# Own buffers for the loads of maxima and of parts, later places for both, and two up-projections ahead of the first scores, in an attention block followed by a mixture of 4096 single-row experts

## The chip, the core and the metric

One core of a Trainium2 chip runs one program. Its engines work side by side and are ordered only by semaphores: PE multiplies matrices (PEld is its weight load), DVE and ACT do element-wise work from the on-chip memories SBUF and PSUM, POOL does element-wise work in SBUF, and SP issues DMA transfers, in order, between device memory and SBUF. The metric is the device time of one execution in microseconds (us).

## The reference, cut to what matters

2048 tokens of 448 features; 16 attention heads of 28; then, for each token and each of 16 heads, the best 8 of 64 x 64 experts, each of which is one row of u (what to multiply with) and one row of v (what to add).

```python
h = x + attention(layernorm(x), wqkv) @ wo
xf = layernorm(h)
q = jnp.einsum("nd,dhc->nhc", xf, w_q)               # two halves, q1 and q2
s1, s2 = q1 . k1, q2 . k2                            # 64 scores each
...                                                  # best 8 of each, then best 8 of the 64 sums
g = _softmax(top_s, axis=-1)
act = _gelu(jnp.einsum("nd,nhkd->nhk", xf, u[top_e]))
h2 = h + jnp.einsum("nhk,nhk,nhkd->nd", g, act, v[top_e])
```

## The kernel before, in words

The 4096 experts are not gathered: all 32 slices of 128 experts are computed for every token, and a dense table G of gate weights picks. Products in fp16 use two planes (a high part and a rest), so each needs 11 matmuls of 128x512 (`mm_all`, line 92, over `products`). u and v are brought to such planes in the kernel: `tops` loads each of the 32 slices (`raw`) and DVE takes its largest absolute value (line 141); `share` makes one scale of them; `part` loads a slice again (`raw`, line 1039), lets POOL scale and split it (`hl`, lines 1044 to 1048) and SP store it (`us` or `vs`, line 1051).

Four stages follow one another.

1. To about 150 us: layer norm, q, k and v (`pq`).
2. Attention, 256 units, one for each of 4 token blocks, 4 groups of 4 heads and 16 key tiles: 12 matmuls S (line 556), two exponentials on ACT (P, line 560), 4 product groups A (line 583). Other work is woven in by `weave`: each generator has a number of steps and a stretch of positions, and the next step is taken from the one whose position is lowest; one position is one unit. The first 68 units carry the folding of the key matrices and `tops` of u. In the second stretch, positions 0 to 189, from about 318 to 843 us (so 2.8 us a position), lie for the token blocks b = 0, 1, 2: the output projection and second layer norm (`project(b)`, positions 5 to 31, 65 to 91, 127 to 153), the expert scores and the best 8 of each (`search(b)`, the 33 positions after; ACT writes the scores to `fresh`, DVE takes maxima and indices, line 809 and 811, into `ti`), then the best 8 of the sums (`pairs_of`, partly on POOL, `sel`, lines 866 to 883; its DVE half is `cand`, `ts`, `pos`). Beside these run the parts of u (positions 0 to 50), the maxima of v (6 to 66), their `share` (67 to 70), and the parts of v (74 to 180). A tile pool keeps so many buffers (`bufs`) for a name; here `raw` has 6, for maxima and parts together.
3. Behind attention, about 843 to 938 us: `project(3)`, the scores of block 3 (`kept_scores`, into `ring`), and G for block 0 (`weights(0)`: DVE makes one-hot tiles `f`, `fg`, `p`, PE sums them, line 1014, ACT copies into G, line 1016). Then `load_X(0)` brings back the layer-normed tokens of block 0.
4. The experts, block after block: `up` (11 matmuls `A<-XHb,u`, line 92, a Gelu into one of four `ring` buffers, line 1170), `weigh` (DVE `ring`, line 1184, ACT `w`, line 1185, DVE `w`, line 1186) and 12 matmuls `acc<-v,w` (line 1211) for each of 32 slices f. Beside block 0 runs `later`: `pairs_of` for what was left of block 2, the best 8 of block 3, then `soften` (`ex`, line 893, `sl`, line 905 and 906), whose `sl` PE transposes (line 917); and then `weights(1)` (line 1004).

In stages 2 and 3 the written order is the order of each engine (`manual_schedule`). In stage 4 a scheduler orders the instructions by its own estimates, so a change of what is ready there moves rows on DVE, ACT and PE.

Of the kernel before, what the change touches and what calls it, by code (L numbers as in the profile page):

```python
# [10 lines left out]
F32 = mybir.dt.float32  # L11
# [17 lines left out]
XS = 2.0 ** 11  # L29
LS = 2.0 ** 11  # L30
TOP = 14
ONE = 2.0 ** 15
QS = 2.0 ** 2 / (XS * 2.0 ** TOP)

# [26 lines left out]
def block(ctx: ExitStack, tc: tile.TileContext, x, wqk, wv, wo, wq, k12, uT, v, cst, out):  # L61
# [565 lines left out]
    X = {}  # L627

    def project(b, offset=6, room=None):

        X[b] = XH, XL = bx.tile([128, 4, 512], F16, name="XHb"), bx.tile([128, 3, 512], F16, name="XLb")
# [80 lines left out]
    PROJECT = 26  # L712

    def load_X(b):
        X[b] = XH, XL = bx.tile([128, 4, 512], F16, name="XHb"), bx.tile([128, 3, 512], F16, name="XLb")
        nc.sync.dma_start(XH, x_d[b][:, :4])
        nc.sync.dma_start(XL, x_d[b][:, 4:])

# [48 lines left out]
    def search(b, order):  # L767


        loads = {}  # L770
        heads = [i for n, (i, j) in enumerate(order) if not n or order[n - 1][0] != i]

        def load(n, k):

            if n < len(heads):
                loads[n, k] = w = sp.tile([128, 4, 4, 128], F16, name="w", bufs=3)
                nc.sync.dma_start(w, wp_d[heads[n]][:, k])

        load(0, 0)
        load(0, 1)  # L780
        load(1, 0)
        yield
        last = None
        g = 0
        for n, (i, j) in enumerate(order):
            if last:
                best(*last)
            turned = n + 1 == len(order) or order[n + 1][0] != i
            src = sp.tile([128, 512], F32, name="fresh", bufs=3)
            nc.scalar.activation(src, scores_of(*X[b], (loads[g, 0], loads[g, 1]), j, turned), AF.Identity, scale=gscale[:, i:i + 1])  # L790
# [233 lines left out]
    def tops(S, src, cols):  # L1024

        raw = {}
        for k in range(36):
            if k < 32:
                raw[k] = sp.tile([128, 512], F32, name="raw", bufs=6)
                nc.sync.dma_start(raw[k][:, :cols], src(k))  # L1030
            if k >= 4:
                S.see(k - 4, raw.pop(k - 4)[:, :cols])
            yield

    TOPS = 36

    def part(S, src, dst, cols, planes):
        raw = sp.tile([128, 512], F32, name="raw", bufs=6)
        nc.sync.dma_start(raw[:, :cols], src)
        yield  # L1040
        yield
        hl = sp.tile([128, planes, 512], F16, name="hl", tag=f"hl{planes}", bufs=5 if planes == 2 else 3)
        r, h = raw[:, :cols], [hl[:, k, :cols] for k in range(planes)]
        nc.gpsimd.tensor_scalar(r, r, S.scale, 1.0, op0=OP.mult, op1=OP.mult)  # L1044
        nc.gpsimd.tensor_copy(h[0], r)
# [25 lines left out]
    with tc.manual_schedule(engines={ET.PE, ET.DVE, ET.Activation, ET.Pool, ET.SP}):  # L1071
# [20 lines left out]
        places = pp.tile([128, 8, 16 * H], F16, name="places", bufs=1)  # L1092
        for k in range(8):
            nc.gpsimd.memset(places[:, k], float(k))
        r2 = ExitStack()
        wo_p = r2.enter_context(tc.tile_pool(name="wo_p", bufs=1, reuse_waits="tile"))
        w2 = r2.enter_context(tc.tile_pool(name="w2", bufs=2, reuse_waits="tile"))
# [3 lines left out]
        for b in range(3):  # L1101
# [24 lines left out]

    us = {}

    def load_u(f):
        u = be.tile([128, 2, 4, 128], F16, name="u")  # L1130
        nc.sync.dma_start(u.rearrange("p k t e -> p k (t e)"), us_d[f])
        return u

    with tc.manual_schedule(engines={ET.PE, ET.DVE, ET.Activation, ET.Pool, ET.SP}):
        room = {"xt": [ring[4 * j + 2] for j in range(4)], "at": [ring[3], ring[7]]}
        pools = [tc.tile_pool(name="sw0", bufs=1, side="right", reuse_waits="tile")]
        with ExitStack() as c1:
            pools = [c1.enter_context(pools[0])]
            sc = kept_scores(3, pools)
            weave((project(3, 2, room), 12, 0, 0.25), (islice(sc, 1), 1, 0.02, 0.03),  # L1140
                  (islice(w0, 8), 8, 0.05, 0.27), (islice(sc, 4), 4, 0.125, 0.29))
            r2.close()
            be = ctx.enter_context(tc.tile_pool(name="be", bufs=3, reuse_waits="tile"))
# [4 lines left out]
            def loads():  # L1148
                store_X(3)
                yield  # L1150
                for f in range(3):
# [4 lines left out]
            load_X(0)  # L1156
    bv = ctx.enter_context(tc.tile_pool(name="bv", bufs=3, reuse_waits="tile"))
    gw = ctx.enter_context(tc.tile_pool(name="gw", bufs=2, side="right", reuse_waits="tile"))
    ring += [bv.tile([128, 512], F32, name=f"ring{i}", bufs=1) for i in range(16, 20)]
    acts = {}  # L1160

    def up(b, f, name):

        XH, XL = X[b]
        u = us.pop(f, None) or load_u(f)
        p = P[0].tile([128, 512], F32, name=name)
        mm_all(p, [(l, r) for r, l in products(lambda t: XH[:, t], lambda t: XL[:, t],
                                               lambda t: u[:, 0, t], lambda t: u[:, 1, t])])
        act = ring[f % 20] if b else ring[16 + f % 4]
        nc.scalar.activation(act, p, AF.Gelu_apprx_tanh, scale=ugelu)  # L1170
        acts[f] = act

    def ups(b, n):
        for f in range(n):
            up(b, f, "M")
# [120 lines left out]
```

## Time and profile before

| | us |
|---|---|
| median of 3 runs | 1605.56 (1604.23 to 1607.88) |
| the profiled execution, its own time | 1608.31 |
| its span, first to last instruction | 1606.5 |
| PE, DVE, ACT, POOL busy | 1538.6, 1145.9, 916.0, 358.4 |
| mean granted PE clock | 0.994 |

The profiled execution stands 2.75 us above the median of the runs, and 1.8 us of its time lie outside the span. "Busy" counts an engine as working from the start to the end of each instruction; matmuls that overlap are joined. A view by windows gives, for each stretch, an engine's busy us with the number of instructions in brackets, and the granted clock, in which 0.50 is half speed. A row of a chain or timeline gives the start, the length, and what ran; an arrow in brackets names what ended the idle time before it. SPq is SP's queue of DMA issues.

### The profile page before, as it was taken

Reading aid. Unit: us, or ns where it says so; the run is one execution under the profiler, and the core shown is the slowest. Engines: PE = TensorE matmul, PEld = TensorE weight load, DVE = VectorE, ACT = ScalarE, POOL = GpSimd, SP = SyncE. Lnnn points to the kernel's source line nnn. Section 1 sums busy time; section 2 is a strip of 40 time slices with the busy share of each in tenths; the row PEclk is TensorE's granted clock in tenths of the full one; section 3 lists DMA queues with packets and bytes.
Section 4 is the critical chain, followed back from the end, with each engine's and each line's share of the span. In section 5 each row is a group of like instructions: output and inputs, shape, how many; then the busy total and the mean of one; then the engine's idle time right before and its main releaser. Section 6 shows DMA issues by size and latency. Waiting matters only on the chain.

```text
span 1606.5 us, 33247 instructions
## 1 busy us (share of the span) xinstructions
PE 1538.6 (96%) x12588; PEld 673.9 (42%) x12588; DVE 1145.9 (71%) x3912; ACT 916.0 (57%) x1220; POOL 358.4 (22%) x488
## 2 busy tenths in 40 slices
PE   5999999999899999999997999899999999999999
PEld 3444222233233333333335654455545554555444
DVE  8763355525477666656598999869999999789732
ACT  3544888878688888988882432433423344334322
POOL 1242000455413576477634000000000000000000
PEclk9999999999999999999999999999999999999999
DMA  8424686577873476457623234444344434554354
GB/s 285 136 95 133 221 272 230 172 233 248 296 227 113 120 241 208 149 174 243 212 71 118 97 115 128 120 146 153 109 135 134 148 120 130 151 156 124 119 153 127
DMA packets 158882, 263.36 MB, mean 164 GB/s; under 512 B 14336, under 2 KB 90880, under 8 KB 158720
## 3 DMA queue, kind: packets, MB, share of 16 engines
q1 hardware_dynamic: 154496, 259.12, 51.2%
q10 hardware_dynamic: 4224, 2.10, 0.4%
q8 instruction: 99, 1.62, 0.4%
q14 instruction: 63, 0.52, 0.1%
HBM read 211.88 MB, written 49.28 MB: 163 GB/s over the span
## 4 chain that ended last, share of the span: by engine, by line
PE 69%; DVE 21%; DMA 4%; POOL 2%; issue 1%; ACT 1%; SPq 0%; DVEq 0%; POOLq 0%; ACTq 0%
PE acc L1211 14%; PE A L583 12%; PE M L92 12%; PE S L556 11%; PE A L92 8%; PE pq L92 6%; DVE p L987 4%; DVE G L1008 2%; DVE ti L811 2%; DVE fg L972 2%; PE M L264 2%; DVE ti L809 1%; PE A L1014 1%; DVE f L966 1%; DMA raw<-in_uT_dram 1%
## 5 line engine op out<-in xcount | busy, mean ns | idle before, releaser
L560 ACT ACTIVATE P<-S,escale 128x1024 f32<-128x1024 f32 x512 | 537.2, 1115 | 91.9 <-PE S L556 85.6
L1211 PE MATMUL acc<-v,w 128*128 128x448 f16 x1536 | 306.0, 352 | 1.6 <-ACT w L1185 0.8
L583 PE MATMUL A<-P,V 128*32 128x512 f32 x2048 | 258.7, 603 | 0.6 <-DVE o L588 0.6
L556 PE MATMUL S<-qS,kS 32*128 32x512 f16 x3072 | 228.8, 380 | 2.9 <-ACT P L560 2.2
L1211 PEld LDWEIGHTS <-w 128*128 128x128 f16 x1536 | 148.1, 98 | 143.1 <-ACT w L1185 3.4
L1185 ACT ACTIVATE w<-ring 128x512 f16<-128x512 f32 x128 | 80.5, 630 | 215.1 <-PE acc L1211 109.3
L92 PEld LDWEIGHTS <-u 128*128 128x128 f16 x1408 | 132.7, 98 | 154.9 <-issue 12.4
L987 DVE TENSOR_TENSOR p<-st,iota 128x2048 f16<-128x2048 f16 x128 | 156.3, 1222 | 7.4 <-PE A L1014 4.1
L92 PE MATMUL A<-XHb,u 128*128 128x512 f16 x568 | 136.1, 382 | 8.0 <-ACT ring L1170 5.6
L556 PEld LDWEIGHTS <-kS 32*128 32x128 f16 x3072 | 62.4, 92 | 192.8 <-issue 158.8
L92 PE MATMUL M<-w,XHb 128*128 128x512 f16 x512 | 128.7, 382 | 6.5 <-DMA w<-wp 4.8
L1186 DVE SCALAR_TENSOR_TENSOR w<-w,ring 128x512 f16<-128x512 f16 x128 | 87.1, 686 | 61.6 <-ACT w L1185 60.9
L1184 DVE SCALAR_TENSOR_TENSOR ring<-ring,wscale,G 128x512 f32<-128x512 f32 x128 | 92.8, 744 | 34.8 <-ACT ring L1170 34.8
L92 PE MATMUL M<-XHb,u 128*128 128x512 f16 x456 | 109.0, 379 | 0.8 <-DVE G L1008 0.8
L583 PEld LDWEIGHTS A<-P,V 128*32 128x32 f32 x2048 | 48.3, 109 | 120.0 <-issue 110.3
L809 DVE MAX8 ti<-fresh 128x8 f32<-128x64 f32 x384 | 57.2, 211 | 57.7 <-ACT fresh L790 57.2
L1170 ACT ACTIVATE ring<-A,ugelu 128x512 f32<-128x512 f32 x71 | 48.6, 684 | 82.9 <-PE A L92 82.9
L1170 ACT ACTIVATE ring<-M,ugelu 128x512 f32<-128x512 f32 x57 | 39.2, 687 | 91.4 <-PE M L92 89.7
L1044 POOL TENSOR_SCALAR raw<-raw,scale 128x512 f32<-128x512 f32 (+1 forms) x64 | 47.0, 734 | 198.5 <-DVE topw L162 147.4
L972 DVE TENSOR_TENSOR fg<-f,st 128x2048 f16<-128x2048 f16 x64 | 78.7, 1229 | 0.1
L811 DVE FIND_INDEX8 ti<-ti,fresh 128x8 uint32<-128x64 f32 x384 | 76.8, 218 | 0.0
L92 PEld LDWEIGHTS <-XHb 128*128 128x128 f16 x512 | 45.3, 98 | 73.3 <-issue 24.9
(196 smaller groups left out, 2069.0 us busy)
## 6 DMA issues: line engine op xcount, KB each, us to landing
v<-vs SPq DMA_DIRECT2D x128, 336.0 KB, 2.9
u<-us SPq DMA_DIRECT2D x128, 256.0 KB, 2.6
w<-wp SPq DMA_DIRECT2D x56, 512.0 KB, 5.2
kS<-ks SPq DMA_DIRECT2D x64, 256.0 KB, 5.0
V<-vd SPq DMA_DIRECT2D x64, 256.0 KB, 3.6
raw<-in_uT_dram SPq DMA_DIRECT2D x64, 256.0 KB, 4.7
wr<-in_wq_dram SPq DMA_DIRECT2D x32, 448.0 KB, 4.2
raw<-in_v_dram SPq DMA_DIRECT2D x64, 224.0 KB, 4.9
```

Source lines behind the costliest of these rows:

```text
L92: nc.tensor.matmul(ps, l, r, start=i == 0, stop=i == len(pairs) - 1)
L556: nc.tensor.matmul(S[j // 2][:, j % 2], kS[r, a, 128 * (k % 4):128 * (k % 4) + 128], qS[r, c], start=m == 0, stop=m == 2)
L560: nc.scalar.activation(Pt[:, 2 * i:2 * i + 2], S[i], AF.Exp, scale=escale[:, n % 4:n % 4 + 1])
L583: nc.tensor.matmul(O[n][32 * j:32 * j + 32], V[:, k % 4, j], Pt[:, j], start=k == 0, stop=k == NT - 1)
L811: nc.vector.max_index(i, t, src)
L972: nc.vector.tensor_tensor(fg.rearrange("p t k f u -> p t k (f u)"), f1.rearrange("p t f u -> p t (f u)").unsqueeze(2).to_broadcast([128, T ...
L987: newest[0] = nc.vector.tensor_tensor(p1, pairs(0, s, TG, 128), ids(TG, 128), op=OP.is_equal).ins
L1170: nc.scalar.activation(act, p, AF.Gelu_apprx_tanh, scale=ugelu)
L1184: nc.vector.scalar_tensor_tensor(av, av, wscale, of_expert(b, f), op0=OP.mult, op1=OP.mult)
L1185: nc.scalar.activation(w[:, 0], a, AF.Copy, scale=1.0 / LS)
L1186: nc.vector.scalar_tensor_tensor(w[:, 1], w[:, 0], -LS, a, op0=OP.mult, op1=OP.add)
L1211: nc.tensor.matmul(acc[j][:, :D], l, r, start=f == 0 and k == 0, stop=f == 31 and k == 2)
```

## The change

Four things are edited. The loads of maxima get buffers of their own, 4 named `seen`, and see each slice 3 steps after its load instead of 4; the parts keep 4 named `raw`, and `hl` of two planes has 4 buffers instead of 5. `fresh` has 2 buffers instead of 3, and the layer-normed tokens `XHb` and `XLb` have 2 instead of 1. The parts of u take positions 0 to 90, the maxima of v 60 to 98, `share` 99 to 102, the parts of v 105 to 186. And slices 0 and 1 of block 0 are projected up in stage 3, between the steps of `project(3)`: their u is loaded into `ring` buffers 11 and 15 at the start of that stage, `load_X(0)` stands at position 166 of attention, and two of the four buffers for the results are made before stage 2 ends.

```diff
-        for k in range(36):
+        for k in range(35):
             if k < 32:
-                raw[k] = sp.tile([128, 512], F32, name="raw", bufs=6)
+                raw[k] = sp.tile([128, 512], F32, name="seen", bufs=4)
                 nc.sync.dma_start(raw[k][:, :cols], src(k))
-            if k >= 4:
-                S.see(k - 4, raw.pop(k - 4)[:, :cols])
+            if k >= 3:
+                S.see(k - 3, raw.pop(k - 3)[:, :cols])
...
     def part(S, src, dst, cols, planes):
-        raw = sp.tile([128, 512], F32, name="raw", bufs=6)
+        raw = sp.tile([128, 512], F32, name="raw", bufs=4)
...
-        work += [(islice(w0, 1), 1, 220 - FOLDED, 221 - FOLDED)]
-        work += [(parts_of_up(7, 32), 25 + PART, 0, 50), (tops(VS, lambda f: v[:, f], D), TOPS, 6, 66), (VS.share(), 3, 67, 70), (scales(), 1, 73, 74),
-                 (parts_of_down(0, 14), 14 + PART, 74, 120), (parts_of_down(14, 32), 18 + PART, 120, 180)]
+        work += [(islice(w0, 1), 1, 220 - FOLDED, 221 - FOLDED), (first_tokens(), 1, 234 - FOLDED, 235 - FOLDED)]
+        work += [(parts_of_up(7, 32), 25 + PART, 0, 90), (tops(VS, lambda f: v[:, f], D), TOPS, 60, 98), (VS.share(), 3, 99, 102), (scales(), 1, 104, 105),
+                 (parts_of_down(0, 32), 32 + PART, 105, 186)]
...
+    def first_up(f):
+        up(0, f, "A")
+        yield
...
+        for f in range(UP0):
+            us[f] = load_u(f, True)
...
-            weave((project(3, 2, room), 12, 0, 0.25), (islice(sc, 1), 1, 0.02, 0.03),
+            weave((project(3, 2, room), 12, 0, 0.25), (first_up(0), 1, 0.025, 0.025), (first_up(1), 1, 0.067, 0.067), (islice(sc, 1), 1, 0.02, 0.03),
...
-        n = AHEAD if b else 0
+        n = AHEAD if b else UP0
```

How this moves instructions is shown at three places. The first is SP's queue at the start of `search(0)`: `raw<-in_v_dram` are loads of maxima, `raw<-in_uT_dram` and `us<-hl` loads and stores of parts, kS and V keys and values, `w<-wp` the weights that the scores of `search` wait for. Before:

```order
L1030 DMA raw<-in_v_dram 128x448 x2
L1051 DMA us_110<-hl 128x1024
L1039 DMA raw<-in_uT_dram 128x512
L213 DMA kS<-ks_64 128x2x512
L225 DMA V<-vd 128x512
L709 DMA xd_86<-XHb 128x2048
L710 DMA xd_86<-XLb 128x1536
L1030 DMA raw<-in_v_dram 128x448
L1051 DMA us_111<-hl 128x1024
L1039 DMA raw<-in_uT_dram 128x512
L777 DMA w<-wp_67 128x2048
L777 DMA w<-wp_68 128x2048
```

Now, with the same two loads of weights at the end:

```order
L1052 DMA us_102<-hl 128x1024
L1040 DMA raw<-in_uT_dram 128x512
L214 DMA kS<-ks_64 128x2x512
L226 DMA V<-vd 128x512
L710 DMA xd_86<-XHb 128x2048
L711 DMA xd_86<-XLb 128x1536
L1052 DMA us_103<-hl 128x1024
L1040 DMA raw<-in_uT_dram 128x512
L778 DMA w<-wp_67 128x2048
L778 DMA w<-wp_68 128x2048
```

Between the same transfers of attention, the loads of maxima are gone, and the stores of parts that stand there are of slices eight numbers lower. The second place is PE at the start of stage 3: `ct,ob` are transposes of the attention output, `ct,o` the last four of attention itself, woh and wol the output projection of the first tile. Before:

```order
L121 MATMUL M<-ct,ob 128x128 x2
L571 MATMUL M<-ct,o 128x128 x4
L121 MATMUL M<-ct,ob 128x128 x6
L92 MATMUL M<-woh,oh_35140 128x448 x4
L92 MATMUL M<-wol,oh_35140 128x448 x4
L92 MATMUL M<-woh,ol_35141 128x448 x3
L1014 MATMUL A<-fg,p_35174 128x32
```

Now, at the same place, with the first matmuls of up-projection 0:

```order
L122 MATMUL M<-ct,ob 128x128 x2
L572 MATMUL M<-ct,o 128x128 x4
L122 MATMUL M<-ct,ob 128x128 x2
L93 LDWEIGHTS ring_35131
L93 MATMUL A<-XHb,ring_35131 128x512
```

and where it ends, up to the first matmul of up-projection 1:

```order
L93 MATMUL A<-XLb,ring_35131 128x512
L122 MATMUL M<-ct,ob 128x128 x4
L93 MATMUL M<-woh,oh_35151 128x448 x4
L93 MATMUL M<-wol,oh_35151 128x448 x4
L93 MATMUL M<-woh,ol_35152 128x448 x3
L93 LDWEIGHTS ring_35135
L93 MATMUL A<-XHb,ring_35135 128x512
```

So 22 of these matmuls stand between the transposes and the projection of the first tile, and behind that. The third place is DVE at the start of stage 4, behind the last one-hot tile of `weights(0)`. Before, ahead of the rows shown stand `cand`, `iv` and two more pairs of MAX and MAX_INDEX of the same kind:

```order
L809 MAX ts_27491<-cand 128x8 x4
L811 MAX_INDEX pos<-ts_27491,cand 128x8 x4
L838 CAST iv<-ti_34422 128x256
L1184 SCALAR_TENSOR_TENSOR ring_36771<-ring_36771,wscale,G 128x512
L846 TENSOR_SCALAR ab<-pos 128x16x8
L847 TENSOR_SCALAR ab<-pos 128x16x8
L809 MAX ti_37135<-ring_35111 128x8
L849 CAST ah<-ab 128x256
L1184 SCALAR_TENSOR_TENSOR ring_36772<-ring_36772,wscale,G 128x512
L1186 SCALAR_TENSOR_TENSOR w<-w,ring_36771 128x512
```

Now, from the first row of that stretch on:

```order
L836 TENSOR_TENSOR cand<-ti_34321 128x1024
L839 CAST iv<-ti_34321 128x256
L810 MAX ts_27491<-cand 128x8 x4
L812 MAX_INDEX pos<-ts_27491,cand 128x8 x4
L1199 SCALAR_TENSOR_TENSOR ring_27507<-ring_27507,wscale,G 128x512
L1199 SCALAR_TENSOR_TENSOR ring_27508<-ring_27508,wscale,G 128x512
L810 MAX ts_27491<-cand 128x8
L1201 SCALAR_TENSOR_TENSOR w<-w,ring_27507 128x512
L1199 SCALAR_TENSOR_TENSOR ring_36804<-ring_36804,wscale,G 128x512
```

The first two `ring` instructions of `weigh` stand behind one group of four maxima and indices instead of four groups. Counted to the row `ex<-ts` (line 893) that ends the maxima of `later`, 16 `ring` and 16 `w` stood before it on DVE, and 18 and 17 now; on PE the first transposes of `sl` stood behind 17 groups of `acc` and 20 up-projections of the block, now behind 17 and 19, the first two not counted; from there to the first matmul of `weights(1)` it is 7 up-projections and 5 groups of `acc` before, 6 and 5 now.

More of the change, by code (lines that the diff above doesn't have):

```diff
@@ L31 @@
 TOP = 14
+UP0 = 2
 ONE = 2.0 ** 15
@@ L629, in project @@
     def project(b, offset=6, room=None):
-        X[b] = XH, XL = bx.tile([128, 4, 512], F16, name="XHb"), bx.tile([128, 3, 512], F16, name="XLb")
+        X[b] = XH, XL = bx.tile([128, 4, 512], F16, name="XHb", bufs=2), bx.tile([128, 3, 512], F16, name="XLb", bufs=2)
         def place(j, name, tag, bufs):
@@ L714, in load_X @@
     def load_X(b):
-        X[b] = XH, XL = bx.tile([128, 4, 512], F16, name="XHb"), bx.tile([128, 3, 512], F16, name="XLb")
+        X[b] = XH, XL = bx.tile([128, 4, 512], F16, name="XHb", bufs=2), bx.tile([128, 3, 512], F16, name="XLb", bufs=2)
         nc.sync.dma_start(XH, x_d[b][:, :4])
@@ L788, in search @@
             turned = n + 1 == len(order) or order[n + 1][0] != i
-            src = sp.tile([128, 512], F32, name="fresh", bufs=3)
+            src = sp.tile([128, 512], F32, name="fresh", bufs=2)
             nc.scalar.activation(src, scores_of(*X[b], (loads[g, 0], loads[g, 1]), j, turned), AF.Identity, scale=gscale[:, i:i + 1])
@@ L1094, in block @@
             nc.gpsimd.memset(places[:, k], float(k))
+        bs = ctx.enter_context(tc.tile_pool(name="bs", bufs=1, reuse_waits="tile"))
+        spare = [bs.tile([128, 512], F32, name=f"ring{i}") for i in range(16, 18)]
         r2 = ExitStack()
@@ L1113, in block, with first_tokens @@
         w0 = weights(0)
[L1114 to L1116 removed]
+        def first_tokens():
+            load_X(0)
+            yield
+        work += [(islice(w0, 1), 1, 220 - FOLDED, 221 - FOLDED), (first_tokens(), 1, 234 - FOLDED, 235 - FOLDED)]
+        work += [(parts_of_up(7, 32), 25 + PART, 0, 90), (tops(VS, lambda f: v[:, f], D), TOPS, 60, 98), (VS.share(), 3, 99, 102), (scales(), 1, 104, 105),
+                 (parts_of_down(0, 32), 32 + PART, 105, 186)]
         weave(*work)
@@ L1127, in block, with load_u, up @@
     us = {}
-    def load_u(f):
-        u = be.tile([128, 2, 4, 128], F16, name="u")
+    def load_u(f, early=False):
+        u = be.tile([128, 2, 4, 128], F16, name="u") if not early else ring[11 + 4 * f].bitcast(F16).rearrange(
+            "p (k t e) -> p k t e", k=2, t=4)
         nc.sync.dma_start(u.rearrange("p k t e -> p k (t e)"), us_d[f])
         return u
+    acts = {}
+    def up(b, f, name):
+        XH, XL = X[b]
+        u = us.pop(f, None) or load_u(f)
+        p = P[0].tile([128, 512], F32, name=name)
+        mm_all(p, [(l, r) for r, l in products(lambda t: XH[:, t], lambda t: XL[:, t],
+                                               lambda t: u[:, 0, t], lambda t: u[:, 1, t])])
+        act = ring[f % 20] if b else spare[f % 4]
+        nc.scalar.activation(act, p, AF.Gelu_apprx_tanh, scale=ugelu)
+        acts[f] = act
+    def first_up(f):
+        up(0, f, "A")
+        yield
     with tc.manual_schedule(engines={ET.PE, ET.DVE, ET.Activation, ET.Pool, ET.SP}):
+        for f in range(UP0):
+            us[f] = load_u(f, True)
         room = {"xt": [ring[4 * j + 2] for j in range(4)], "at": [ring[3], ring[7]]}
@@ L1150, in loads @@
                 yield
-                for f in range(3):
+                for f in range(UP0, UP0 + 3):
                     us[f] = load_u(f)
@@ L1155, in block @@
             weave((w0, WEIGHTS - 9, 0.29, 1), (sc, 13, 0.29, 0.92), (loads(), 4, 0.6, 0.8))
-            load_X(0)
     bv = ctx.enter_context(tc.tile_pool(name="bv", bufs=3, reuse_waits="tile"))
     gw = ctx.enter_context(tc.tile_pool(name="gw", bufs=2, side="right", reuse_waits="tile"))
[L1159 to L1171, printed above, removed]
+    spare += [bv.tile([128, 512], F32, name=f"ring{i}", bufs=1) for i in range(18, 20)]
+    ring += spare
     def ups(b, n):
```

4 lines of the change are left out of this document (2 added, 2 removed).

## Prediction

> **What bounds the kernel now.** The first view is the page's list of busy times: PE works 96% of the span, so a change gains only where PE waits or runs at half clock, and costs only where it makes new waits.
>
> ```profile
> PE 1538.6 (96%) x12588; PEld 673.9 (42%) x12588; DVE 1145.9 (71%) x3912; ACT 916.0 (57%) x1220; POOL 358.4 (22%) x488
> ```
>
> The second is a table by windows, cut where the change works: start and end, length, then busy us (instructions) of PE, PEld, DVE, ACT and POOL, the granted clock, DMA share, GB/s.
>
> ```profile
> 318.00:342.00 24.00, 21.22 (x216) 5.43 (x208) 9.12 (x20) 22.35 (x22) 7.19 (x8) 1.00 0.69 213
> 342.00:408.60 66.60, 63.00 (x575) 23.59 (x579) 28.93 (x56) 50.11 (x48) 40.51 (x54) 0.97 0.76 248
> 408.60:474.35 65.75, 60.96 (x518) 19.13 (x514) 38.87 (x288) 49.28 (x50) 21.82 (x27) 0.97 0.82 269
> 508.00:591.20 83.20, 81.61 (x762) 29.27 (x763) 56.69 (x266) 68.99 (x67) 48.32 (x68) 1.00 0.54 169
> 600.00:800.00 200.00, 199.46 (x1798) 66.86 (x1790) 121.78 (x779) 170.87 (x176) 129.53 (x184) 1.00 0.62 197
> 839.00:880.00 41.00, 30.21 (x300) 20.57 (x293) 35.15 (x84) 14.45 (x25) 20.41 (x29) 0.92 0.33 106
> 937.80:1024.30 86.50, 79.64 (x380) 36.92 (x377) 85.89 (x560) 25.84 (x38) 0.00 (x0) 0.98 0.41 117
> ```
>
> PE idles in three places: 2.78 + 3.60 + 4.79 = 11.17 us in the first three rows, where parts of u and maxima of v run together; 10.79 us at the start of stage 3; 6.86 us at the start of stage 4, where DVE works 85.89 of 86.50 us. The 200 us of the fifth row have no gain in them (0.54 us idle). The clock was halved here, by a finer table of the same kind:
>
> ```profile
> 343.70:347.10 3.40, 3.40 (x21) 1.48 (x23) 1.43 (x3) 0.21 (x1) 3.16 (x5) 0.50 0.14 54
> 435.90:439.20 3.30, 3.19 (x16) 0.70 (x15) 0.57 (x5) 0.69 (x1) 0.05 (x1) 0.50 1.02 364
> 937.70:941.00 3.30, 3.30 (x13) 1.13 (x10) 3.30 (x29) 1.88 (x2) 0.00 (x0) 0.50 0.15 54
> ```
>
> Each costs half its length, 1.7 us. Why the first place waits is in the waits from 300 to 520 us (engine and line, what it waited for: us in total, times, longest) and in the chain of work that ended last there (start, length, what ran):
>
> ```profile
> SPq L1039 <- POOL hl L1046: 15.2, 6, 3.7
> SPq L1030 <- POOL hl L1046: 14.5, 7, 3.4
> PE M L92 <- DMA w<-wp: 4.8, 2, 3.0
> PE M L92 <- DVE oh L128: 2.9, 1, 2.9
> ```
>
> ```profile
> 414.35 1.17 POOL hl L1046
> 415.54 0.33 SPq L1039
> 415.96 5.15 DMA w<-wp
> 421.16 1.04 PE M L92 x4
> ```
>
> SP issues in order. A load into `raw`, of a part (L1039) or of a maximum (L1030), waits until POOL has split the part that held the buffer, 29.7 us of waits in all; the weights `w<-wp` of `search(0)` stand behind it and reach PE late.
>
> **The change part by part.** *A, the first place.* With own buffers and the maxima gone from positions 6 to 59, loads of maxima no longer wait for POOL there, and 25 parts spread over 90 positions instead of 50 come at 0.56 of the rate, so that a buffer is free when its next load comes. At best all 11.17 us and two half clocks of 1.7 go: 14.6. What stays: `project(1)`, the fourth row, has the same work without this jam and idles 1.59 us; and the weights of the output projection still come in transfers of 6.34 us between POOL steps in the first row, for which I keep 2.0. So A = −(14.6 − 3.6) = **−11**, between −14.6 and −4.8 (only PE's waits for `w<-wp`, the third row of the waits, go).
>
> ```profile
> 333.85 6.34 DMA wor<-in_wo_dram
> ```
>
> *B, two up-projections.* One costs PE 2.37 us, by the chain of waits in a stretch of stage 4 where PE never stops:
>
> ```profile
> 1172.33 2.37 PE A L92 x11
> ```
>
> In stage 3 they stand where PE waits. What sets the end there is POOL: it had to finish the last `sel` work before the layer norm's `rstd`.
>
> ```profile
> 828.42 4.11 POOL L870 TENSOR_TENSOR sel<-sel 128x1024 f16<-128x1024 f16 x3
> 847.05 5.30 POOL L870 TENSOR_TENSOR sel<-sel 128x1024 f16<-128x1024 f16 x3
> 856.82 1.05 POOL L109 TENSOR_SCALAR rstd<-mv 128x1 f32<-128x1 f32 x1
> ```
>
> Until 856.8 the 4.74 us are covered by the 10.79 idle. Their two loads of u and the two of `load_X(0)` are issued earlier on SP, where the loads are fewer now; if the u is late, PE waits with the projection behind it. I put **+0.5** (0 with the cover, 4.74 without it).
>
> In stage 4 the order puts the first `ring` instructions of `weigh` behind one group of maxima instead of four. These rows of the timelines (start, length) show the stretch:
>
> ```profile
> 939.36 0.58 DVE L809 MAX8 ts<-cand 128x8 f32<-128x64 f32 x4
> 944.98 0.75 DVE L1184 SCALAR_TENSOR_TENSOR ring<-ring,wscale,G 128x512 f32<-128x512 f32 x1 [0.25 <-ACT ring L1170]
> 946.59 0.68 DVE L1186 SCALAR_TENSOR_TENSOR w<-w,ring 128x512 f16<-128x512 f16 x1
> 946.43 2.43 PE L1211 MATMUL acc<-v,w 128*128 128x448 f16 x12
> 1020.95 0.67 DVE L893 TENSOR_TENSOR ex<-ts 128x512 f32<-128x512 f32 x1
> 1025.16 0.28 DVE L906 TENSOR_TENSOR sl<-ex,sl 128x128 f16<-128x128 f32 x1
> 1033.62 0.28 PE L917 MATMUL M<-ident,sl 128*128 128x128 f16 x2
> 1062.86 0.64 PE L1004 MATMUL M<-fg,p 128*128 128x64 f16 x16
> ```
>
> A first `ring` at 939.36 and 2.3 us from it to `w` (944.98 to 947.27 in the second) make the first `acc` possible at 941.7 instead of 946.43. But DVE is full until `ex`, and its order has two `ring` and one `w` more before that: 2 x 0.65 + 0.6 (starts apart) = 1.9, so `ex` starts at 1022.85. From `ex` to the first `sl` it is 4.4 us, so PE's transposes can start at 1027.25, 6.37 before 1033.62, if PE has its 17 groups and 17 up-projections done: 17 x (2.27 + 2.37) from 937.7 end near 1018, so DVE and not PE sets it. From there to line 1004 it is one up-projection less, 2.37. Together 8.74; 0.6 off for a first `acc` that PE waits for at half clock: **−8.1**, between −0.5 (PE's rows keep their distance from `ex`, which is 1.9 later, and one up-projection of 2.37 is gone) and −11.6 (6.86 idle and 4.74 of work, all gone).
>
> *C, the maxima of v beside `project(1)`.* By the trace a maximum takes 0.647 us:
>
> ```profile
> L141 DVE TENSOR_REDUCE tops<-raw x64: 585/647/683, 175.7 to 511.6; 128x1 f32<-128x512 f32 x32, 128x1 f32<-128x448 f32 x32
> ```
>
> 32 of them are 20.7 us over 38 positions of 2.8, 106 us; of these 83.2 lie in the fourth row, so DVE there goes from 56.69 to 72.9, from 68% to 88%. The layer norm of `project` waits for DVE, and the wait for `oh` (2.9) is such a wait. At 59% (third row) PE idled 4.79, though from the jam, at 99% (last row) 6.86 in 86.5. I take **+3**, nearly half of that last row, between 0 and +6.9. The loads move with them, to a row with a DMA share of 0.54 from rows with 0.76 and 0.82, so I add nothing for transfers.
>
> *D, the parts of v in 81 positions instead of 106.* In the 200 us window POOL's groups for parts were (count, busy us, mean ns, idle before):
>
> ```profile
> L1046 POOL TENSOR_TENSOR hl<-raw,hl 128x448 f16<-128x448 f32 x25 | 26.0, 1040 | 2.1
> L1044 POOL TENSOR_SCALAR raw<-raw,scale 128x448 f32<-128x448 f32 x24 | 17.7, 738 | 9.0 <-DMA raw<-in_v_dram 8.6
> L1048 POOL TENSOR_SCALAR hl<-hl 128x448 f16<-128x448 f16 x25 | 14.6, 583 | 0.0
> L1045 POOL CAST hl<-raw 128x448 f16<-128x448 f32 x24 | 13.4, 557 | 22.5 <-DMA vs<-hl 21.3
> ```
>
> 71.7 us; at 106/81 of the rate 22 more, POOL 129.5 to 152 of 200, 76%. Nobody on PE waits for parts then, unless SP's queue jams again: **+0.5**, between 0 and +22 (the third row's 4.79 + 1.7 in 65.75 us, kept up over 225).
>
> *E, buffers.* Two `fresh` instead of three: ACT writes the next but one only when DVE has searched the buffer. At the end of `search(2)` the two met:
>
> ```profile
> 830.59 0.69 ACT L790 ACTIVATE fresh<-M,gscale 128x512 f32<-128x512 f32 x1 [0.34 <-PE M L92]
> 830.85 0.22 DVE L811 FIND_INDEX8 ti<-ti,fresh 128x8 uint32<-128x64 f32 x1
> ```
>
> DVE's last index of a buffer ends at 831.07, 0.48 after ACT's start; over the few places like that **+0.5** (0 to 2). Second buffers for `XHb` and `XLb`, and 4 `hl` instead of 5 at a slower rate, cost nothing that I see: stores and loads at 0.56 of the rate cover them.
>
> Sum: −11 + 0.5 − 8.1 + 3 + 0.5 + 0.5 = **−14.6**. Against the profiled execution's own 1608.31 this is 1593.7; that execution stood 2.75 above the median, so the median comes to **1591.0**.
>
> **Rules of the skill against it.** The clock dropped around waits of 2.9 and 3.0 us. The Trainium skill ("TensorE: Matmul & The Clock Gate", What's actually happening) grants half clock only after a whole idle window of about 3.4 us; by that, no short wait earns a half clock, and the 3.4 us in A would stay: 1594.4. The trace agrees in the length (3.3 to 3.4 us) and not in the cause, so I keep my credit. And the Trainium skill ("GPSIMD Engine Reference", Key points) says that POOL shares its SBUF interfaces with VectorE, and suffers from DVE instructions with two SBUF inputs; the same three L870 took 4.11 and 5.30 us here, which agrees. It speaks against C and D, whose room is above.
>
> **Rivals.** (1) DVE gives B back: with 88 and 99% it lets PE do the early `acc` and then wait, as at 1024.33; B shrinks to its −0.5 and the time is 1598.6. For it: 85.89 of 86.50. Against: the first `sl` was ready at 1025.44, 8.2 us before PE took it. (2) A stays small or C is dear: −4.8 instead of −11, and up to +6.9 instead of +3; 1597.2 to 1601.1. For it: DMA share 0.76 to 0.82, which transfers of attention alone could hold up. (3) The change does not do what it says: four `raw` for the parts still block the queue, A is nothing and C +6.9 against a B of −8.1; 1591.0 + 11 + 3.9 = 1605.9, the same as before. For it: the parts now have fewer buffers than the six of before. (4) Slower: the jam moves to `search(1)` and `search(2)`, since the 32 parts of v share SP's queue with `w<-wp`; +22 instead of +0.5, and A unchanged, gives 1612. It decides once PE idles by more than 0.07 us in each us of that stretch (15.1 of other gains over 225), against 0.54 in 200 us now; SP's longest waits for POOL there, from 600 to 800 us, are in this row, so it is far off:
>
> ```profile
> SPq L1051 <- POOL raw L1044: 1.9, 3, 0.8
> ```
>
> (5) All gains in full and C at nothing: 1583.
>
> **How the numbers follow.** My forecast has 0.55, with a range of its own of 1586 to 1597; rival 1 has 0.17, rival 2 0.13, rival 3 0.05, rival 4 0.06, rival 5 0.04. The likeliest gives 1591.0. The range, 1583 to 1602, reaches from rival 5 over rivals 1 and 2 and leaves out 3 and 4 and the tails. A difference below 0.2% (3.2 us) can't be told from none: faster takes all cases up to 1602.3, which are the forecast, rivals 1, 2 and 5, less 0.03 for their tails: 0.86; same is rival 3 with that tail, 0.08; slower is rival 4, 0.06.
>
> **What would show it.** Right: from 318 to 474 us no wait of PE for `w<-wp`, SP's waits for POOL under 5 us, a clock of 1.00; two groups of 11 matmuls `A<-XHb` between 844 and 860, with the end of stage 3 no later against the end of attention; the first `acc` about 4.7 us closer to the last matmul of `weights(0)`, and line 1004 about 8 closer. Wrong: PE idle above 5 us in `project(1)` with DVE near 90%; SP waiting for POOL beside `search(1)` or `search(2)`; `ex` later than 3 us against the end of `weights(0)`; PE waiting for u in stage 3.

## The result, and the profile after

The changed kernel takes 1601.37 us (median of 21 runs, 1597.58 to 1607.25), the kernel before 1607.67 us (21 runs, 1604.23 to 1611.54). The ratio is 0.996, with a 95% interval of 0.9951 to 0.9968: faster by 0.4%. Forecast was 1591.0 with a range of 1583 to 1602. The sign is right and the time lies within the range, at its upper edge; the gain is 6.3 us, not 14.6. The profiled execution of the changed kernel took 1602.62 us, with a span of 1600.8, so the two profiled executions differ by 5.7 us. Executions of one kernel differ by up to 11 us here, and the mean granted clock of the changed kernel's runs lies between 0.990 and 0.996: how much of a run falls on half clock varies, and each stretch of half clock (3.41 us in the trace) is worth 1.7 us.

The first stretch is what was forecast. The page's busy times, and the first three windows (start and end, length, busy us of PE, PEld, DVE, ACT, POOL, granted clock, DMA share, GB/s):

```profile
PE 1540.3 (96%) x12588; PEld 675.1 (42%) x12588; DVE 1146.7 (72%) x3912; ACT 914.7 (57%) x1220; POOL 358.4 (22%) x488
```

```profile
318.00:342.00 24.00, 22.81 (x223) 7.36 (x224) 8.99 (x19) 21.47 (x22) 7.00 (x7) 1.00 0.63 202
342.00:408.60 66.60, 65.58 (x624) 23.07 (x623) 24.37 (x67) 55.35 (x54) 27.95 (x38) 1.00 0.55 181
408.60:474.35 65.75, 65.73 (x581) 21.04 (x577) 39.29 (x325) 54.74 (x57) 16.62 (x21) 1.00 0.62 201
```

PE idles 1.19 + 1.02 + 0.02 us instead of 11.17, and the clock is full. No load waits for POOL in SP's queue from 300 to 520 us, where the waits were 29.7 us. What the gain was lost to is seen when both timelines are cut at the same events. The table gives the length of each stretch in us, worked out from the timelines of the profiled executions: from the starts of the first and the last row of projection matmuls `M<-woh,oh` of `project(1)`, of the first and the last `fresh` of `search(2)` and of the first matmul of `weights(1)` (line 1004, now 1005), and from the ends of the last `A<-P,V` of attention, of the last `A<-fg,p` of `weights(0)` and of the span.

| stretch | before | after | difference |
|---|---|---|---|
| start to `project(1)` | 515.75 | 502.88 | −12.87 |
| `project(1)` | 45.80 | 48.26 | +2.46 |
| from there to `search(2)` | 185.37 | 186.57 | +1.20 |
| `search(2)` | 89.89 | 94.74 | +4.85 |
| end of attention to the end of `weights(0)` | 94.42 | 95.59 | +1.17 |
| from there to the first matmul of `weights(1)` | 125.03 | 122.41 | −2.62 |
| from there to the end | 543.64 | 543.75 | +0.11 |

The 6.60 us between the last `fresh` and the end of attention are the same in both. Of the first row, 0.87 us lie ahead of position 0 (318.63 and 317.76 us): the execution before had a half clock at 159.37 us, at the start of attention, that this one has not. It is no part of the change: the last kernel below has the changed buffers and a half clock there. The change is thus worth 12.0 us in this row.

**`search(2)`.** The waits of PE from 750 to 850 us have a row that this place did not have before, and the chain of work shows what PE waited for; below it SP's issues of the same moment (start, length, what was issued):

```profile
PE M L93 <- DMA w<-wp: 3.0, 1, 3.0
```

```profile
776.85 2.48 PE M L93 x11
779.33 0.35 PE S L557 x5
779.67 7.61 DMA w<-wp
787.28 0.04 issue
787.32 1.02 PE M L93 x4
```

```profile
776.15 0.32 SPq L226 DMA_DIRECT2D V<-vd  x1
776.52 0.42 SPq L717 DMA_DIRECT2D XHb<-xd  x1
776.99 1.30 SPq L718 DMA_DIRECT2D XLb<-xd  x1
778.39 0.53 SPq L1052 DMA_DIRECT2D vs<-hl  x1
778.96 0.62 SPq L1040 DMA_DIRECT2D raw<-in_v_dram  x1
779.67 0.97 SPq L778 DMA_DIRECT2D w<-wp  x2
```

The weights were issued when their buffer came free, 0.3 us after the matmuls that had it, yet took 7.61 us to land. Ahead of them stands `load_X(0)`, which the change had moved into attention: 512 + 384 KB; between the two, a store and a load of parts, 336 + 224 KB. PE waited 3.0 us, and a half clock followed (0.70 on average from 787.30 to 790.10).

**`project(1)`.** The chain ahead of PE's longest wait there runs through DVE, with three of the moved maxima (`tops`) in it:

```profile
523.56 0.69 DVE o L589
524.25 0.53 DVE tops L142
...
526.82 1.05 DVE tops L142 x2
527.88 1.74 DVE cand L836
529.62 0.30 DVE iv L839
529.94 0.70 DVE oh L648
...
531.68 0.63 PE M L572 x4
```

PE waited 2.41 us at 531.68, where it had waited 1.57 before, and this time a half clock followed. The row of before, and the window behind the wait now:

```profile
543.70 0.63 PE L571 MATMUL M<-ct,o 128*128 128x128 f32 x4 [1.57 <-DVE oh L128]
```

```profile
533.00:536.40 3.40, 3.40 (x28) 0.64 (x20) 3.40 (x27) 0.00 (x0) 1.77 (x2) 0.59 0.00 0
```

**Block 0.** The timelines of PE, ACT and DVE at the places that were shown of before (start, length, what, and in brackets the idle time ahead and what ended it):

```profile
1000.71 3.22 PE L93 MATMUL A<-XHb,u 128*128 128x512 f16 x8 [3.57 <-ACT ring L1153]
1024.56 3.24 PE L93 MATMUL A<-XHb,u 128*128 128x512 f16 x8 [3.30 <-ACT ring L1153]
1030.56 0.27 PE L918 MATMUL M<-ident,sl 128*128 128x128 f16 x2
1057.05 0.64 PE L1005 MATMUL M<-fg,p 128*128 128x64 f16 x16
1020.59 1.28 ACT L896 ACT_TABLE_LOAD   x1
1021.88 0.63 ACT L896 ACTIVATE ex<-ex 128x512 f32<-128x512 f32 x1
1022.53 1.28 ACT L1153 ACT_TABLE_LOAD   x1
1023.82 0.69 ACT L1153 ACTIVATE ring<-A,ugelu 128x512 f32<-128x512 f32 x1
1021.04 0.68 DVE L894 TENSOR_TENSOR ex<-ts 128x512 f32<-128x512 f32 x1
1024.67 0.23 DVE L906 CAST sl<-ex 128x128 f16<-128x128 f32 x1
```

```profile
934.64:1021.04 86.40, 82.50 (x390) 38.87 (x389) 84.91 (x557) 22.05 (x36) 0.00 (x0) 0.96 0.41 116
```

The first `acc` came 4.66 us after the end of `weights(0)` instead of 8.60, as the order promised. But PE idled 7.26 us in this stretch, as before (7.34), now nearly all of it in two waits of over 3 us (eight matmuls after each took 3.22 and 3.24 us, where they take 1.89 at full clock), and its transposes (`M<-ident,sl`) came 5.9 us after the first `sl`, not at once. PE's busy time fell by 2.54 us: 4.74 of work were gone, and some 2.2 came back as slower matmuls. Two of the waits before, at full clock behind them:

```profile
1005.37 1.89 PE L92 MATMUL A<-XHb,u 128*128 128x512 f16 x8 [1.05 <-ACT ring L1170]
1024.33 1.89 PE L92 MATMUL A<-XHb,u 128*128 128x512 f16 x8 [2.55 <-ACT ring L1170]
```

### The profile page after: what moved, and what is told of

Same layout as the page of the kernel before. It is cut to its first block, busy times and chain, and to the rows that moved or that the text cites. A ratio compares the mean times of both kernels' runs of the same rounds, so it can differ in the third digit from the quotient of the medians.

```text
span 1600.8 us, 33230 instructions
## 1 busy us (share of the span) xinstructions
PE 1540.3 (96%) x12588; PEld 675.1 (42%) x12588; DVE 1146.7 (72%) x3912; ACT 914.7 (57%) x1220; POOL 358.4 (22%) x488
## 4 chain that ended last, share of the span: by engine, by line
PE 72%; DVE 21%; DMA 2%; ACT 1%; POOL 1%; issue 1%; SPq 0%; DVEq 0%; ACTq 0%; POOLq 0%
PE acc L1226 14%; PE A L584 14%; PE M L93 13%; PE S L557 12%; PE A L93 8%; PE pq L93 6%; DVE p L988 4%; DVE G L1009 2%; DVE ti L812 2%; DVE fg L973 2%; PE M L265 2%; DVE ti L810 1%; PE A L1015 1%; DVE f L967 1%; DVE pos L812 1%
## 5 line engine op out<-in xcount | busy, mean ns | idle before, releaser
L93 PEld LDWEIGHTS <-XHb 128*128 128x128 f16 x512 | 45.4, 97 | 69.3 <-issue 21.9
```

What stands on the lines that cost most here:

```text
L93: nc.tensor.matmul(ps, l, r, start=i == 0, stop=i == len(pairs) - 1)
```

## Experiments

Each time is the median of 5 to 12 runs, beside a kernel before at 1607.6 to 1607.8; "stretch" refers to the table above.

**Taking the up-projections out.** In stage 3:

```
-UP0 = 2
+UP0 = 0
-  (first_up(0), 1, 0.025, 0.025), (first_up(1), 1, 0.067, 0.067),
```

> The change without its two up-projections in stage 3 (UP0 = 0); load_X(0) stays at position 166. Theory DVE: block 0 is bound by VectorE up to `ex`, so the two up-projections saved only 2.6 us there and cost 1.2 in stage 3; without them the time is 1.4 us above the changed kernel, some 1602.8, and from the end of weights(0) to line 1005 it takes 125.0 us again. Rival (the up-projections gave their 8 us, and half clock in this one profile hid it): 1608, and that stretch is 130.

It took 1604.79 us, ratio 0.9977 (0.9966 to 0.9988), so 3.4 above the change by the medians (2.7 by the two ratios), and the stretch of block 0 was 125.41, as before the change. The up-projections are worth something between the two theories, nearer to the first.

**`load_X(0)` between the searches.**

```
-  (first_tokens(), 1, 234 - FOLDED, 235 - FOLDED)
+  (first_tokens(), 1, 140, 141)
```

> The change with load_X(0) at position 140 instead of 166, between the searches. Theory queue: the one wait for w<-wp at 787 us (3.0 us and a half clock of 1.7) comes from the 0.9 MB of load_X(0), issued 2.7 us ahead of those weights; it goes, and search(2) gets back 4.7 us: 1596.7. Rival POOL: the wait comes from the parts of v at their higher rate, whose stores hold SP's queue; then it stays, and the time is that of the change, 1601.4.

1596.77 us, ratio 0.9934 (0.992 to 0.9948). `search(2)` took 90.00 us instead of 94.74, PE no longer waited for `w<-wp` there, and the parts of v ran at the same rate. The transfers of `load_X(0)`, not POOL, made the wait. In the kernel without up-projections and in the next two, which load it at 166 as well, `search(2)` took 95.7 to 96.9.

**`later` over 0.70 of block 0, with and without up-projections.**

```
-SPLIT = (0.58, 0.5, 0.3)
+SPLIT = (0.7, 0.5, 0.3)
```

> The change with `later` spread over 0.70 instead of 0.58 of block 0 (SPLIT). Theory DVE: VectorE falls below 90% there, PE's 7.2 us of waits and two half clocks (3.4) go from block 0: about 8 us less, 1593. Rival: the work is only moved; `sl` and weights(1) come later, and PE waits for them at the end of block 0: 1601 or above.

> Both: UP0 = 0 and `later` over 0.70 of block 0. Theory DVE: with VectorE off the path the two up-projections are worth their 4.74 us of PE work and the earlier first `acc`, less 1.2 in stage 3, so this is 5 to 7 us above the kernel with 0.70 and two up-projections (1598 to 1600), where at 0.58 the difference is 1.4. Rival: the difference stays at 1 to 2 us.

1608.45 us, ratio 0.9997 (0.9981 to 1.0013), and 1611.34, ratio 1.0012 (0.9998 to 1.0027). The edit did not do what I meant. This window of the kernel with two up-projections begins at the end of its `weights(0)`:

```profile
938.79:1024.79 86.00, 80.05 (x391) 38.15 (x389) 85.83 (x559) 23.14 (x37) 0.00 (x0) 0.99 0.40 117
```

DVE is as full as before: in stage 4 the scheduler placed the work of `later` as early as it had, whatever its share; `ex` comes 85.2 us after the end of `weights(0)`, 86.4 in the change. Only the transposes moved, 20 us later, and the work behind them with them. This pair says nothing on DVE's part in PE's waits.

**Positions alone, buffers alone.** The kernel before with the new positions, and the kernel before with only `seen` and `raw` apart (4 and 4, each slice seen 3 steps after its load), 4 `hl` and 2 `fresh`:

```
+ (parts_of_up(7, 32), 25 + PART, 0, 90), (tops(VS, ...), TOPS, 60, 98), (VS.share(), 3, 99, 102), ...
+ (parts_of_down(0, 32), 32 + PART, 105, 186)
```

> The kernel before with the new positions alone (parts of u 0 to 90, maxima of v 60 to 98, share 99 to 102, parts of v 105 to 186); six shared buffers, no up-projection and no load_X(0) moved. Theory positions: they alone clear the jam beside project(0) and search(0); the start of project(1) comes 12.9 us earlier as in the changed kernel, project(1) gives 2.5 back and search(2) nothing, about 1597.5. Rival buffers: loads still wait for POOL in the shared buffers, the start of project(1) comes at most 5 us earlier, and the time is 1603 or more.

1603.17 us, ratio 0.9977 (0.9966 to 0.9988). The start of `project(1)` came 11.94 us earlier, as the theory had it, but `project(1)` took 48.06 and the way to `search(2)` 186.53, as in the change.

```
- raw[k] = sp.tile([128, 512], F32, name="raw", bufs=6)
+ raw[k] = sp.tile([128, 512], F32, name="seen", bufs=4)
- raw = sp.tile([128, 512], F32, name="raw", bufs=6)
+ raw = sp.tile([128, 512], F32, name="raw", bufs=4)
```

> The kernel before with the buffers alone: 4 `seen` for maxima, 4 `raw` for parts, 4 `hl` of two planes, 2 `fresh`; the old positions. Theory positions: loads of maxima no longer wait for POOL, but the maxima still take the wires beside project(0) and search(0); project(1) starts 3 to 6 us earlier than before, 1602 to 1605. Rival buffers: they alone take away the 12.9 us, 1595. Second rival: four `raw` hold SP's queue as six did, no difference, 1607.6.

1598.34 us, ratio 0.9941 (0.9928 to 0.9955): my theory fell, its rival was right. The same three windows of this kernel:

```profile
318.00:342.00 24.00, 22.82 (x224) 6.74 (x223) 9.43 (x22) 22.55 (x22) 8.49 (x10) 1.00 0.69 226
342.00:408.60 66.60, 65.59 (x615) 23.56 (x615) 32.01 (x81) 54.51 (x53) 44.63 (x59) 1.00 0.87 287
408.60:474.35 65.75, 65.73 (x573) 21.02 (x574) 45.13 (x333) 54.60 (x56) 18.20 (x24) 1.00 0.78 259
```

Its DMA share is 0.87 and 0.78, as high as before, and PE idles 1.18 + 1.01 + 0.02. So the transfers never were too many; only their queue stood still: no load waits for POOL in it from 300 to 520 us. Eight buffers stand here in place of six, and no run gave eight shared ones; whether the separation or the number did it is not shown. `project(1)` takes 45.78 and the way to `search(2)` 185.38, as before. Positions and buffers each take away the same 12 us, and the positions cost 3.4 on top (2.28 + 1.15, in the profiled executions). Two `fresh` cost nothing that can be seen: the searches of this kernel are as long as before.

**Maxima of v beside `search(0)`.**

```
-  (tops(VS, lambda f: v[:, f], D), TOPS, 60, 98)
+  (tops(VS, lambda f: v[:, f], D), TOPS, 32, 64)
```

> The change with load_X(0) at 140 and the maxima of v at positions 32 to 64, beside search(0), instead of 60 to 98 beside project(1). Theory VectorE: the 2.5 us that project(1) lost go back to it, and search(0) stays as it is: 1594.3. Rival: search(0), whose best 8 VectorE takes, waits instead, by 2 to 5 us, or the transfers there make w<-wp late again: 1597 to 1600.

1596.21 us, ratio 0.9939 (0.9927 to 0.9951). `project(1)` took 45.43 instead of 49.51, and `search(0)` lost nothing (`project(1)` began at 503.37). That settles that the maxima are what `project(1)` paid for. How much depends on the clock: with the change's buffers and the maxima at 60 to 98 it took 46.6 us in two kernels where no half clock fell on it, 48.0 to 48.3 in five with one, and 49.5 with two, against 45.4 to 45.8 without them there. The time did not show the gain, since stage 3 took 98.32 us in the profiled execution: PE waited 0.61 us for u (`ring<-us`), and half clock fell on it in two places, 10.2 us in all.

**Less work for DVE in block 0.** `load_X(0)` at 140, and the last 8 of the 32 steps of `bests` left out, with and without up-projections:

```
+ if j == 3: ti[j] = bk.tile(...); nc.gpsimd.memset(ti[j], 0.0)
  for i in range(8):
-     best(i, j, kept(i, j))
+     if j < 3: best(i, j, kept(i, j))
```

> The change with load_X(0) at 140, and with the search of the last quarter of block 3 left out (zeros stand in for its best 8), which takes some 10.3 us of VectorE from block 0. Theory VectorE: from the end of weights(0) to line 1005 it takes 122.4 us in the changed kernel, of which 7 are waits of PE and 3.4 half clock; 7 to 10 us go, 1587 to 1590. Rival: PE waits there for the exp of `later` with its two table loads on ACT and for the order of its own queue; at most 3 us go, 1594 or more.

> The same, with the search of the last quarter left out, and without the two up-projections in stage 3. Theory VectorE: with VectorE off the path each up-projection in stage 3 takes its 2.37 us out of block 0, so this is 4 to 5 us slower than the kernel with them, against 3.4 with full VectorE. Rival: 1 to 2 us slower, since block 0 has room now.

1598.05 us, ratio 0.9943 (0.993 to 0.9956), and 1603.3, ratio 0.997 (0.9958 to 0.9982). `ex` started 71.4 us after the end of `weights(0)` instead of 85.9 (the kernel with the whole search and `load_X(0)` at 140), and still the stretch of block 0 took 121.54 us, no less than that kernel's 120.52. PE's two waits are in it, the first at the same distance from the end of `weights(0)` (64.5 us, 66.1 in the change):

```profile
997.50 2.91 PE L93 MATMUL A<-XHb,u 128*128 128x512 f16 x8 [3.66 <-ACT ring L1157]
1007.80 2.96 PE L93 MATMUL A<-XHb,u 128*128 128x512 f16 x8 [3.80 <-ACT ring L1157]
```

So taking 10 us of DVE's work out ahead of `ex` does not take these waits away: the theory fell in this form. On the first wait the run says less than it seems, since the work left out stood behind it: from the third on, the distances between DVE's `ring` instructions up to there are those of the changed kernel, to 0.02 us. The second wait came earlier together with `ex`: it ends 3.4 us after the start of `ex` here (1004.42), 3.5 in the changed kernel and 3.4 before. What the timelines show of the first is DVE's pace. In the changed kernel these are the first and the last of 14 `ring` instructions of `weigh` on DVE, one for each slice:

```profile
955.64 0.73 DVE L1199 SCALAR_TENSOR_TENSOR ring<-ring,wscale,G 128x512 f32<-128x512 f32 x1
...
1024.82 0.74 DVE L1199 SCALAR_TENSOR_TENSOR ring<-ring,wscale,G 128x512 f32<-128x512 f32 x1
```

Over 13 distances that is 5.32 us for a slice, with about 12 maxima and their indices between two of them, while PE needs 4.64 us for an `up` and an `acc`; ACT's Gelu stands behind the `w` that waits for `ring`, and PE's next `up` behind Gelu. PE loses its lead of a few slices and then waits. The first wait, up to 1000.71, falls where 16 maxima stand between two `ring` instead of 12 (992.30 to 998.68):

```profile
998.68 0.73 DVE L1199 SCALAR_TENSOR_TENSOR ring<-ring,wscale,G 128x512 f32<-128x512 f32 x1
999.45 0.63 ACT L1200 ACTIVATE w<-ring 128x512 f16<-128x512 f32 x1 [5.18 <-DVE ring L1199]
999.98 0.67 ACT L1153 ACTIVATE ring<-A,ugelu 128x512 f32<-128x512 f32 x1
```

In the kernel before the distances there are 5.7 to 5.9 us, 1.0 to 1.3 over PE's 4.64, and PE waited 1.05, 1.13 and 0.88 us in three slices in a row. That the pace is the cause of the first wait is what the spacing says; no run changed the spacing alone. The two up-projections are worth 5.2 us here, by the medians, as the theory of the second run had it, though PE did wait for DVE.

**The exponential beside `ex`.** A copy in its place, in blocks 2 and 3 of the tokens, `load_X(0)` at 140:

```
- nc.scalar.activation(ex, ex, AF.Exp)
+ nc.scalar.activation(ex, ex, AF.Exp if b < 2 else AF.Identity)
```

> The change with load_X(0) at 140, and with the exponential of `soften` in the last two uses replaced by a copy, which leaves out two table loads of 1.28 us on ACT beside `ex` in block 0; PE's order is the same. Theory ACT: PE's second wait in block 0 (3.30 us at 1024.56 in the changed kernel) is Gelu's wait behind these loads; it falls below 1 us, its half clock goes, and from the end of weights(0) to line 1005 it is 2.5 to 4.5 us less: 1593. Rival VectorE: the wait is for `ring` on VectorE, whatever ACT does; it stays over 2.5 us, 1596.8.

1594.85 us, ratio 0.9918 (0.9905 to 0.9932), 1.9 less than with the exponential, which the intervals hardly tell apart. The stretch of block 0 was 118.19 instead of 120.52, and the second wait shrank to

```profile
1017.71 1.89 PE L93 MATMUL A<-XHb,u 128*128 128x512 f16 x8 [1.76 <-ACT ring L1153]
```

from 2.38 in the kernel with it. Of the 2.33 us that the stretch lost, only 0.42 are idle time of PE; the rest is less time at half clock. Neither theory is right alone: the table loads carry a part of that wait, most of it remains. What remains stands at the same place in ACT's order, where the copy waits for DVE's `ex` and the Gelu (1016.99) stands behind the copy:

```profile
1016.46 0.63 ACT L896 ACTIVATE ex<-ex 128x512 f32<-128x512 f32 x1 [1.19 <-DVE ex L894]
```

No run put that Gelu ahead of `ex`.

**Better versions.** First the maxima at 32 to 64 and the up-projections later in stage 3:

```
-  (first_up(0), 1, 0.025, 0.025), (first_up(1), 1, 0.067, 0.067)
+  (first_up(0), 1, 0.067, 0.067), (first_up(1), 1, 0.13, 0.13)
```

> Maxima of v at 32 to 64, load_X(0) at 140, and the two up-projections later in stage 3: the first behind the projection of the first tile, the second behind one-hot sums. Theory cover: PE then waits for no u and works where it waited 2.0 us for `xn`, so from the end of attention to the end of weights(0) it is 94 to 95.6 us instead of 98.3: 1593 to 1595. Rival: the waits of stage 3 move with it, 1596 as before.

1595.49 us, ratio 0.9918 (0.9905 to 0.9932); stage 3 took 95.31. Then the change's buffers with the old positions, `load_X(0)` at 140, and the up-projections at those later places:

```
-  (parts_of_up(7, 32), 25 + PART, 0, 90), (tops(VS, ...), TOPS, 60, 98), (VS.share(), 3, 99, 102), ...
+  (parts_of_up(7, 32), 25 + PART, 0, 50), (tops(VS, ...), TOPS, 6, 66), (VS.share(), 3, 67, 70), ...
```

> What the runs so far speak for: the change's own buffers with the old positions of parts and maxima, load_X(0) at 140, and the two up-projections later in stage 3. Theory: buffers alone gave 9.4 us, the up-projections without load_X(0) in search(2) some 3.5 more: 1594 to 1595. Rival: old positions and up-projections collide (the old ones end the parts of v at 180, so none should), or stage 3 gives it back: 1597 or more.

1593.59 us, ratio 0.9915 (0.9899 to 0.9932), the fastest of all, though not told apart from the one above. `project(1)` takes 45.77, `search(2)` 90.10, stage 3 94.60 and the stretch of block 0 121.18: the change's gains without the prices that it paid in `project(1)` and `search(2)`. PE's two waits of over 3 us in block 0 are still there.

## Why the prediction was right and wrong

- **The base.** The profiled execution, from which the sum starts, was taken to stand 2.75 us above the median of 3 runs; above the median of 21 it stands 0.64. So 2.1 of the 10.4 us between forecast and time come from the base, and 8.3 from the terms. The time lies in the range because rivals 1 and 2 had widened it; no rival had `load_X(0)`, which cost most, so this is luck in part.
- **A, the jam: right.** Forecast −11, measured −12.0 (−12.87 less the 0.87 ahead of position 0); no wait of PE for `w<-wp`, SP's waits for POOL 3.3 us, and full clock from 318 to 474 us. That it took both the buffers and the positions was wrong: either alone does it.
- **C, maxima beside `project(1)`: right in kind, the size partly by luck.** Forecast +3, measured +2.46. DVE stood in front of PE as told, but PE's idle time grew only from 1.57 to 2.41 us, with DVE busy for 78% of `project(1)`, not 88; the rest is a half clock of 1.7, which the forecast did not give to C. Maxima moved away took it back.
- **D and E:** forecast +0.5 each. The way from `project(1)` to `search(2)` is 1.2 longer, and it is so in every kernel with the new positions of the parts, also where the maxima stand at 32 to 64, and in none with the old; the buffers E cost nothing that can be seen.
- **The step that failed first: "Their two loads of u and the two of `load_X(0)` are issued earlier on SP, where the loads are fewer now".** I listed these transfers and priced only a late u in stage 3, which did not come; `load_X(0)` had no price. Position 166 lies in `search(2)`, whose weights, 512 KB each, are issued in pairs some 12 us apart; 0.9 MB in front of a pair cost 4.85: a wait of 3.0 and a half clock of 1.7. Weights held up in `search(2)` are the mechanism of rival 4, here once, from another transfer than the parts of v.
- **The step that failed second, in B: "so DVE and not PE sets it".** I let PE reach its transposes near 1018 (17 x 4.64 from 937.7 is 1016.6) and then wait for `sl`. PE's up-projections do not run free there: each waits for Gelu, which waits behind `w` for `ring` on DVE, and at the end behind `ex` with its two table loads as well. `ex` itself came 3.3 us later against the end of `weights(0)` (86.40 and 83.12), forecast was 1.9. PE kept its 7.3 us of waits, and got two half clocks behind them. B was −2.62 against −8.1 here, and about −4 over the kernels that leave block 0 as it is: with up-projections this stretch took 122.41, 120.52, 120.74, 120.67 and 121.18, mean 121.1, and without them 125.03, 125.41, 124.88 and 124.89, mean 125.05. That is a little less than their 4.74 us of work, taken out of block 0. The earlier first `acc` (3.94) is in no sum: PE waits for it later. Rival 1 had this, at a price of 1598.6 with `load_X(0)` at nothing.
- **Stage 3:** forecast +0.5, measured +1.17. Among all kernels this stretch took 94.4 to 98.3 us, with no order between those with and those without up-projections: 4.74 us of work more did not show, so the cover was there, and this is as much as one can say.
- **The clock:** I took 3.4 us of half clock out of A and gave the other terms none, but for 0.6 in B. The waits at 531.68 and 787.32 and the two in block 0 each brought one. By the Trainium skill ("TensorE: Matmul & The Clock Gate", What's actually happening) half clock comes after at least one idle window of about 3.4 us. The traces agree with the length and not with the need for a whole idle window. Half clock begins on a grid: in the changed kernel at 532.40, 788.40, 856.67, 931.76, 1000.03 and 1023.92, which are 75, 20, 22, 20 and 7 times 3.413 us apart. What counts, by these traces, is how much of a wait falls into one slot of that grid. The wait of 2.41 lay wholly in one; the wait of 2.55 in the kernel before, behind which the clock stayed full, lay across two. The slot of the first, and the two of the second, by windows:

```profile
528.99:532.40 3.41, 1.00 (x16) 0.57 (x12) 2.52 (x6) 2.19 (x3) 3.07 (x6) 1.00 0.70 255
```

```profile
1019.54:1022.95 3.41, 2.25 (x12) 1.08 (x11) 3.12 (x14) 2.26 (x3) 0.00 (x0) 1.00 0.37 89
1022.95:1026.36 3.41, 2.02 (x10) 0.96 (x10) 3.31 (x11) 2.41 (x4) 0.00 (x0) 1.00 0.28 94
```

PE idled 2.41 of 3.41 us in the one, 1.16 and 1.39 in the others; ahead of the other three half clocks it was 2.3 (787.32), 2.9 and 2.7 us. In the fourteen traces, from 160 us on, all 31 slots in which PE idled 2.0 us or more had half clock behind them; with less, some had and some had not.

## What to carry to other kernels

Before spacing work out to relieve a queue that issues in order, see whether its head waits for a buffer: buffers of their own for work with different consumers, eight in place of six, took away 12 us at the full rate of transfers, at no price in time that can be seen, while spreading the work moved it in front of something else. A load that is moved early is to be priced against whichever load with a deadline stands behind it in the new place. And an instruction that may start earlier gains nothing where the engine waits later for the pace of another; what it does gain is the work that it takes from there.

## What the runs showed of the hardware

A weight load of 512 KB took 7.61 us to land behind 0.9 MB of `load_X(0)` and 0.56 MB of parts, where the median is 5.2 us. Waits of PE gathered in one piece cost more than the same time in pieces: in block 0 the kernel before waited 7 us in pieces of at most 2.55 with no half clock behind them, and the changed kernel 7.3, nearly all in two of over 3 us, and lost some 1.3 us more after each, eight matmuls taking 3.2 us instead of 1.89. Half clock came in slots of 3.41 us on a fixed grid, and which wait brought it depended on where the wait lay on the grid: 2.41 us inside one slot did, 2.55 us across two did not.
